# Moving the four state products of group 0 one period later, next to those of group 1

## The chip, the cores and the metric

The kernel runs on one core of a Trainium2 chip. The metric is the device time of one execution in microseconds (us). A profile comes with one execution; its span (first to last instruction) is shorter than the time of the same execution (for example 795.4 and 797.42). PE is the matmul engine, PEld its weight loads, DVE the vector engine, ACT the activation engine, POOL the general engine, and SP the engine that issues the DMAs.

## The reference, cut to what matters

The program is a pre-norm attention with a running memory, followed by a gated MLP. The attention works in 4 segments of 512 tokens and 32 heads of width 32:

```python
for s in range(N):
    p = softmax(qs @ ks^T * scale + mask); a_dot = p @ vs
    a_mem = (phi(qs) @ M) / (phi(qs) @ z + 1e-06)
    outs.append(g * a_mem + (1 - g) * a_dot)
    M = M + phi(ks)^T @ vs          # the "state products"
    z = z + phi(ks).sum(rows)
```

The state products of segment s are used first in segment s+1. The kernel takes 8 groups of 4 heads per segment; one step of the main loop, here "period n", makes the logits of group n, the P·V products and the state products of group n-1, and the Q and K projections of group n+1. So group 0's state products have about six periods (over 45 us) before anybody needs them.

## The kernel before: what the change touches

Instructions go to one queue per engine in the order in which they are recorded. A helper derives the waits; every instruction is issued from one of its lines, which is why the profile says L209 everywhere. It tracks PSUM by whole bank, SBUF in cells of 32 bytes. PQK holds phi(Q) and phi(K) of a group; PK (pk in the profile) is phi(K) after a DMA transpose, and it is the weights of the state products. The logits of a group are made in three rounds, 0 to 2; ACT takes the exp of each round and POOL applies the causal mask. The layer norm's rstd (rs in the profile) is made on POOL too.

```python
MSUM = cb("msum", [128, NQ, 132], F32)
PVX = PS[:, 4:6, :]...[:, 0:688]        # P.V results: bank 4 and columns 0..175 of bank 5
STB = PS[:, 5, 176:308]                 # state products, bank 5
# [...] head of the program: the last loads before the loop, all on SP's one queue
for tc in range(4, 8):
    x_load(tc)
sp.dma_start(WK[:, :, 256:D], wcols(A_wk, 256, D))     # 1.5 MB
sp.dma_start(WQ[:, :, 256:D], wcols(A_wq, 256, D))     # 1.5 MB
phi_exp(0)
phi_max(0)                              # ends with the DMA transpose PK[0] <- PQK[0]
# [...]
def pv(n, cqs=range(4)):
    # [...] P.V matmuls
    if 3 in cqs:
        state(n)                        # 4 matmuls, weights PK[n % 3]
        norm(n)                         # DVE: reads banks 4 and 5, then state_sum(n)
# [...]
def state_sum(n):
    # [...]
    if s == 0:
        dve.tensor_copy(MSUM[:, c, :], STB)
    # [...] three POOL operations: mask with g, fold into MZB
# [...] period n
logits(n, 0); fill(f1)                  # f1: K projection of group n+1
if n > 0: pv(n - 1, range(3))
logits(n, 1)
if n > 0: pv(n - 1, (3,))               # last P.V part, then state and norm
bg_pop()                                # layer-norm statistics on DVE
fill(f2)                                # Q projection of group n+1, and its eviction on DVE
logits(n, 2)
```

The softmax here doesn't subtract the row's maximum and nothing guards it: scores larger than these inputs give would overflow.

## Time and profile before

| | before |
|---|---|
| time, median of the first 3 runs | 796.97 us (796.62 to 797.53) |
| span of the profile | 795.4 us |
| PE busy | 784.7 us |
| DVE busy | 380.0 us |
| one steady period of segment 0 | 7.60 us |

These are lines of the page of the kernel before: the span, the busy time by engine, and the chain of waits by engine and by line.

```profile
span 795.4 us, 13019 instructions
...
PE 784.7 (99%) x5565; PEld 378.3 (48%) x5657; DVE 380.0 (48%) x745; ACT 295.6 (37%) x347; POOL 173.8 (22%) x329
...
PE 94%; DVE 3%; DMA 2%; issue 1%
```

PE bounds the kernel. The chain in order of time (start, duration, what) shows one long piece that is not PE:

```profile
12.30 7.25 PE ps L209 x33
19.55 10.92 DMA pk<-pqk
30.98 7.55 PE ps L209 x83
...
38.59 7.55 PE ps L209 x83
```

The 10.92 us are the time from issue to landing of the transpose of pk of group 0. They are not lost time: PE works under most of them. What is lost is read from the timeline of PE (start, duration, engine, line, operation, output and inputs, count, idle time before):

```profile
29.19 0.57 PE L209 MATMUL ps<-v,e 128*128 128x33 bf16 x16
30.52 0.41 PE L209 MATMUL ps<-v,pk 128*128 128x132 bf16 x4 [0.76 <-DMA pk<-pqk]
30.98 1.67 PE L209 MATMUL ps<-xnT,wq 128*128 128x512 bf16 x7
...
37.72 0.56 PE L209 MATMUL ps<-v,e 128*128 128x33 bf16 x16
38.14 0.40 PE L209 MATMUL ps<-v,pk 128*128 128x132 bf16 x4
...
42.25 0.39 PE L209 MATMUL ps<-qk 32*128 32x512 bf16 x4
```

In period 2 the state products start 0.42 us after the last P·V part. In period 1 it is 1.33 us, so 0.91 us are lost. Two lines of period 2 show how close DVE is to PE (the Q eviction, then the weight load of the first logits of period 3, which need it):

```profile
41.46 0.64 DVE L209 TENSOR_TENSOR qk<-ps,rb 128x512 bf16<-128x512 f32 x1
...
42.24 0.10 PEld L209 LDWEIGHTS ps<-qk 32*128 32x128 bf16 x4 [0.42 <-DVE qk L209]
```

The eviction ends at 42.10 and PE goes on at 42.25. The 0.42 us is idle time of PEld, not of PE: the matmuls of the V projection run until then.

### The profile page before, as it was taken

To read this page: it belongs to the slowest core of one execution; us is meant where nothing else is said; L and a number is where in the kernel's file an instruction comes from. 1 tells how busy PE (TensorE), PEld (TensorE's weight loads), DVE (VectorE), ACT (ScalarE), POOL (GpSimd) and SP (SyncE) were. 2 spreads that over 40 slices of the span, in tenths; PEclk is the share of its full clock that TensorE was granted. 3 is DMA by queue.
4 is the path that set the end of the run, shared out by engine and by line. 5 is a ranking of instruction groups with operands and counts; after the bars stand their busy time and mean duration, and the time that the engine had idled before them with its cause. 6 is when DMAs were issued, how large, how long until landed. Compare 5 with 4: busy or idle time off the path is not lost.

```text
span 795.4 us, 13019 instructions
## 1 busy us (share of the span) xinstructions
PE 784.7 (99%) x5565; PEld 378.3 (48%) x5657; DVE 380.0 (48%) x745; ACT 295.6 (37%) x347; POOL 173.8 (22%) x329
## 2 busy tenths in 40 slices
PE   8999999999999999999999999999999999999998
PEld 3445455554554455455544444444444444444444
DVE  7664689679954765744562000053234323323332
ACT  5777877887787675133333333100000000000000
POOL 4554565566553331100230000000000000000000
DMA  9762555353415425411116000640270143021003
GB/s 296 175 160 60 94 81 121 87 103 84 110 22 126 114 65 136 125 47 54 54 54 132 1 1 0 220 92 7 79 133 1 33 108 78 1 59 54 1 7 86
DMA packets 125002, 64.83 MB, mean 82 GB/s; under 512 B 94992, under 2 KB 113936, under 8 KB 124944
## 3 DMA queue, kind: packets, MB, share of 16 engines
q1 hardware_dynamic: 124944, 63.99, 33.7%
q8 instruction: 44, 0.72, 0.4%
q14 instruction: 14, 0.11, 0.1%
HBM read 32.51 MB, written 8.39 MB: 51 GB/s over the span
## 4 chain that ended last, share of the span: by engine, by line
PE 94%; DVE 3%; DMA 2%; issue 1%
PE ps L209 94%; DMA pk<-pqk 1%; DVE stats L209 1%; DMA xch<-in_A_x_dram 0%; DVE hch L209 0%; DVE otok L209 0%; DVE lno L209 0%; DVE pqk L209 0%; DVE ta L209 0%; DVE xnT L209 0%; DVE rd L209 0%; DVE mv L209 0%; DVE etmp L209 0%; DVE rdm L209 0%; DVE upd L209 0%
## 5 line engine op out<-in xcount | busy, mean ns | idle before, releaser
L209 PE MATMUL ps<-wspT,z 128*128 128x512 bf16 x878 | 193.1, 379 | 0.9
L209 ACT ACTIVATE e<-ps 128x2048 bf16<-128x2048 f32 (+1 forms) x96 | 152.7, 1590 | 42.4 <-PE ps L209 42.3
L209 PEld LDWEIGHTS ps<-wspT,z 128*128 128x128 bf16 x896 | 87.7, 98 | 105.7
L209 DVE TENSOR_TENSOR tmpg<-ps,brow 128x512 f32<-128x512 f32 x56 | 38.7, 691 | 196.7 <-DMA brow<-in_B_b_sp_dram 103.7
L209 POOL TENSOR_SCALAR_AFFINE_SELECT e<-e 128x512 bf16<-128x512 bf16 x128 | 90.3, 717 | 126.2 <-ACT e L209 125.9
L209 PE MATMUL ps<-win,hnT 128*128 128x448 bf16 x512 | 98.4, 352 | 0.0
L209 PE MATMUL ps<-w_out,yT 128*128 128x512 bf16 (+2 forms) x453 | 96.9, 372 | 0.5
L209 PE MATMUL ps<-hnT,win 128*128 128x512 bf16 x439 | 96.2, 379 | 0.5
L209 PEld LDWEIGHTS ps<-win,hnT 128*128 128x128 bf16 x512 | 49.7, 98 | 46.4 <-issue 0.2
L209 PEld LDWEIGHTS ps<-w_out,yT 128*128 128x128 bf16 x462 | 44.7, 98 | 52.3
L209 PEld LDWEIGHTS ps<-hnT,win 128*128 128x128 bf16 x448 | 43.8, 98 | 52.8
L209 PE MATMUL ps<-xnT,wk 128*128 128x512 bf16 x234 | 59.6, 380 | 1.2
L209 PE MATMUL ps<-wv,xnT 128*128 128x512 bf16 x255 | 59.2, 380 | 0.3 <-ACT xnT L209 0.2
L209 ACT ACTIVATE z<-ps 128x448 bf16<-128x448 f32 x60 | 32.5, 543 | 69.4 <-PE ps L209 69.4
L209 PE MATMUL ps<-wo,oT 128*128 128x512 bf16 x254 | 57.7, 379 | 0.1
L209 ACT ACTIVATE z1T<-ps 128x512 bf16<-128x512 f32 x56 | 33.4, 597 | 63.3 <-PE ps L209 63.3
L209 DVE TENSOR_TENSOR fin<-fin,ps 128x512 bf16<-128x512 bf16 (+2 forms) x33 | 22.2, 671 | 71.3 <-DMA fin<-out_dram 39.9
L209 PE MATMUL ps<-xnT,wq 128*128 128x512 bf16 x225 | 53.9, 379 | 1.8 <-issue 0.2
L209 DVE BATCH_NORM_STATS2 zst<-z 128x6 f32<-128x448 bf16 x64 | 38.9, 620 | 30.1 <-ACT z L209 30.1
L209 PEld LDWEIGHTS ps<-v,e 128*128 128x128 bf16 x1280 | 38.8, 96 | 14.0 <-issue 6.5
L209 PE MATMUL ps<-v,e 128*128 128x33 bf16 x1280 | 42.2, 178 | 0.0
L209 DVE TENSOR_TENSOR yT<-tmpg,z1T 128x512 bf16<-128x512 f32 x56 | 38.8, 692 | 1.9
(86 smaller groups left out, 611.8 us busy)
## 6 DMA issues: line engine op xcount, KB each, us to landing
xch<-in_A_x_dram SPq DMA_DIRECT2D x16, 256.0 KB, 3.5
xr<-in_A_x_dram SPq DMA_DIRECT2D x16, 256.0 KB, 4.0
out_dram<-hch SPq DMA_DIRECT2D x16, 256.0 KB, 2.4
fin<-out_dram SPq DMA_DIRECT2D x16, 256.0 KB, 2.8
out_dram<-fin SPq DMA_DIRECT2D x31, 128.0 KB, 1.7
win<-in_B_w_in_dram SPq DMA_DIRECT2D x4, 896.0 KB, 5.1
w_out<-in_B_w_out_dram SPq DMA_DIRECT2D x1, 3584.0 KB, 12.8
win<-in_B_w_in_dram SPq DMA_DIRECT2D x3, 1024.0 KB, 5.1
```

What stands on the lines that cost most here:

```text
L209: ins = getattr(e, op.name)(*op.args, **op.kw)
```

## The change

The intent is to let PE do other work where it waits for pk of group 0. The four matmuls, their copy out of PSUM and three POOL operations move from period 1 to period 2, behind those of group 1. Group 0's results get columns of their own (the same bank 5 nevertheless). The stride of MSUM grows to a multiple of 32 bytes, so that neighbouring groups share no cell.

```diff
-    MSUM = cb("msum", [128, NQ, 132], F32)
+    MSUM = cb("msum", [128, NQ, 136], F32)
-    STB = PS[:, 5, 176:308]
+    STB = [PS[:, 5, o:o + 132] for o in (176, 308)]
 # pv
         if 3 in cqs:
-            state(n)
+            if n:
+                state(n)
+            if n == 1:
+                state(0)
             norm(n)
 # norm
-        state_sum(n)
+        if n:
+            state_sum(n)
+        if n == 1:
+            state_sum(0)
 # state, state_sum: STB becomes STB[n == 0]; MSUM[:, c, :] becomes MSUM[:, c, 0:132]
 # [...]
```

More of the change, by code (lines that the diff above doesn't have):

```diff
@@ L606, in state @@
         for tcl in range(4 if s < NSEG - 1 else 0):
-            pe.matmul(STB, PK[n % 3][:, tcl, :], V[:, tcl, 4 * c:4 * c + 4, 0:33], start=(tcl == 0), stop=(tcl == 3))
+            pe.matmul(STB[n == 0], PK[n % 3][:, tcl, :], V[:, tcl, 4 * c:4 * c + 4, 0:33], start=(tcl == 0), stop=(tcl == 3))
     def state_sum(n):
@@ L613, in state_sum @@
         if s == 0:
-            dve.tensor_copy(MSUM[:, c, :], STB)
+            dve.tensor_copy(MSUM[:, c, 0:132], STB[n == 0])
         else:
-            dve.tensor_copy(UPD[n % 2][:], STB)
-            pool.tensor_tensor(MSUM[:, c, :], MSUM[:, c, :], UPD[n % 2][:], ALU.add)
-        pool.tensor_tensor(DGM[:], MSUM[:, c, :].rearrange("p (i d) -> p i d", d=33), MASKG[:, c, :, :], ALU.mult)
+            dve.tensor_copy(UPD[n % 2][:], STB[0])
+            pool.tensor_tensor(MSUM[:, c, 0:132], MSUM[:, c, 0:132], UPD[n % 2][:], ALU.add)
+        pool.tensor_tensor(DGM[:], MSUM[:, c, 0:132].rearrange("p (i d) -> p i d", d=33), MASKG[:, c, :, :], ALU.mult)
         pool.tensor_tensor(HALF2[:], DGM[:, 0:2, :], DGM[:, 2:4, :], ALU.add)
```

## The prediction

> **What bounds the kernel now.** TensorE: the page has PE busy 784.7 of 795.4 us, and the chain of waits is 94% PE. A steady period of segment 0 lasts 7.60 us, 7.55 of them matmuls back to back. One piece of the chain that is not PE is large: "DMA pk<-pqk", 10.92 us from 19.55. It does not cost 10.92 us, as PE works under nearly all of it. The timeline of PE in period 1 has P·V of group 0 (last part) at 29.19, its state products only at 30.52 (released by DMA pk<-pqk), the Q projection at 30.98. One period later P·V to state takes 0.42 us (37.72 to 38.14). So the stall is 1.33 - 0.42 = 0.91 us.
>
> The transpose of pk is issued at 19.55 and lands 10.9 us later (median of all 24: 2.4), behind 1.5 MB loads of wk and wq on the same queue; wq lands at 29.2. The Trainium skill, "DMA: Bandwidth & Descriptors", section "Two DMAs through the same engine are not ordered", says that within one queue of an engine descriptors start in order; 10.9 against 2.4 us agrees.
>
> **What the change does.** Four matmuls move from period 1 to just behind those of group 1 in period 2, where both transposes have long landed (30.5 and 31.0, against 38). Nothing is added on PE. Their DVE copy (0.28 us, 0.20 start to start) and three POOL operations (1.16 us together) move along. The results get columns of their own, in the same PSUM bank 5. The stride 136 ends false sharing between neighbouring groups, which costs no wait now.
>
> - Period 1: the 0.91 us stall goes; 0.45 us of products move on (neutral).
> - New limits there: the Q projection could start at 29.63; wq landed at 29.20. Round-2 logits would be ready at 31.25; the exp that frees their banks ends at 31.19. Close; I allow 0.05 us.
> - Period 2: the normalisation waits for both products (the kernel guards PSUM by bank), as PE's next work does; but DVE makes two copies, +0.20 us, ahead of the Q eviction that gates the next logits. In a steady period that eviction ends at 42.10 and the logits start at 42.25: hardly any slack. Estimate: 0.12 us of new stall (0.05 to 0.2).
> - POOL: +1.16 us in period 2 delays the round-2 mask to about 43.9 (needed after 45) and the layer-norm rstd by 0.7 us; both have slack.
>
> Net: -0.91 + 0.05 + 0.12, about -0.7 us. What follows starts earlier by as much, as loads are issued by engine progress.
>
> **Predicted:** 796.2 us, range 795.3 to 797.2; faster by over 2%: 0.005, within 2%: 0.99, slower: 0.005.
>
> **What would show each step.**
> 1. No idle of PE by DMA pk<-pqk; the chain loses that piece.
> 2. P·V of group 0 to Q projection in period 1: about 0.45 us, not 1.79.
> 3. In period 2 eight state matmuls in a row, about 0.85 us, and two msum copies.
> 4. First logits of period 3 at 41.5 to 41.7 instead of 42.25; later periods 7.60 us as before, the shift constant to the end.
> 5. PEld waits for "DVE qk" 0.1 to 0.2 us longer there.
>
> **What would make it wrong.** The wq load landing after 29.6: the Q projection takes over the wait, gain under 0.5 us. The DVE delay lasting over more periods, as DVE is nearly in step with PE: gain near 0. Run spread (796.62 to 797.53) exceeds the effect, so medians may hide it. An error in bank 5 would show in the result, not in the time.

## The result

| | before | after |
|---|---|---|
| time, median of 6 runs | 796.79 us (796.33 to 797.53) | 796.80 us (796.49 to 797.13) |
| ratio | | 1.0000, 95% interval 0.9987 to 1.0013 |
| span of the profile | 795.4 us | 795.1 us |

A ratio is the mean time of one kernel's fast runs over that of the other's of the same rounds, so not quite the ratio of the medians. The interval is 1 us wide on either side: the predicted -0.7 us lies inside it, and so does zero. The times alone can't decide; the profile must be read.

Page of the kernel after:

```profile
span 795.1 us, 13111 instructions
...
PE 789.9 (99%) x5657; PEld 378.4 (48%) x5657; DVE 379.3 (48%) x745; ACT 295.6 (37%) x347; POOL 172.1 (22%) x329
...
PE 96%; DMA 2%; DVE 1%; ACT 0%; SPq 0%; issue 0%
```

(PE "busy" is 5 us higher, but 92 more matmul records are in this trace, 5657 against 5565, while both have 5657 weight loads: records are missing before, it is not more work.) The chain, in order of time:

```profile
14.85 0.04 issue
14.89 15.18 DMA wq<-in_A_wq_dram
30.06 0.04 issue
30.11 11.79 PE ps L209 x108
```

The timeline of PE, the same places as before:

```profile
29.42 0.56 PE L209 MATMUL ps<-v,e 128*128 128x33 bf16 x16
30.11 1.90 PE L209 MATMUL ps<-xnT,wq 128*128 128x512 bf16 x8
...
37.08 0.57 PE L209 MATMUL ps<-v,e 128*128 128x33 bf16 x16
37.49 0.63 PE L209 MATMUL ps<-v,pk 128*128 128x132 bf16 x8
37.96 1.89 PE L209 MATMUL ps<-xnT,wq 128*128 128x512 bf16 x8
...
41.94 0.40 PE L209 MATMUL ps<-qk 32*128 32x512 bf16 x4
```

And DVE and PEld in period 2:

```profile
39.27 0.49 DVE L209 COPY msum<-ps 128x132 f32<-128x132 f32 x2
...
41.25 0.64 DVE L209 TENSOR_TENSOR qk<-ps,rb 128x512 bf16<-128x512 f32 x1
...
41.93 0.10 PEld L209 LDWEIGHTS ps<-qk 32*128 32x128 bf16 x4 [0.53 <-DVE qk L209]
```

Three things are seen. The wait for pk is gone. In its place the Q projection of period 1 waits for the wq load: it starts 0.69 us after the last P·V part, where 0.41 us would be free of waits. And in period 2 the Q eviction comes later relative to PE, so that the first logits of period 3 wait for it.

For all further comparisons the span is cut into three parts: the **head** H, from the start to the last P·V part of group 0 (29.19 before, 29.42 after); the **middle** M, from there to the first logits of period 3 (42.25 - 29.19 = 13.06 before, 41.94 - 29.42 = 12.52 after); the **tail**, the rest (753.13 in both, from the ends of the spans before they are rounded). The change acts on the middle only, where it won 0.54 us in this pair of profiles. The head, where both kernels are the same instruction for instruction, was 0.23 us longer; the heads of all 14 profiles below spread over 28.99 to 29.72. The tail is the same to 0.01 us: nothing is given back later.

### The profile page after: what moved, and what is told of

Its sections match the earlier page's. It is cut to its first block, busy times and chain, and to the rows that moved or that the text cites. A ratio compares the mean times of both kernels' runs of the same rounds, so it can differ in the third digit from the quotient of the medians.

```text
span 795.1 us, 13111 instructions
## 1 busy us (share of the span) xinstructions
PE 789.9 (99%) x5657; PEld 378.4 (48%) x5657; DVE 379.3 (48%) x745; ACT 295.6 (37%) x347; POOL 172.1 (22%) x329
## 4 chain that ended last, share of the span: by engine, by line
PE 96%; DMA 2%; DVE 1%; ACT 0%; SPq 0%; issue 0%
PE ps L209 96%; DMA wq<-in_A_wq_dram 2%; DMA xch<-in_A_x_dram 0%; DVE stats L209 0%; ACT junk L209 0%; DVE xnT L209 0%; DVE lno L209 0%; SPq L209 0%; ACT xnT L209 0%; DVE mv L209 0%; DVE fin L209 0%
## 5 line engine op out<-in xcount | busy, mean ns | idle before, releaser
L209 PE MATMUL ps<-xnT,wq 128*128 128x512 bf16 x256 | 60.6, 379 | 0.1
```

Source lines behind the costliest of these rows:

```text
L209: ins = getattr(e, op.name)(*op.args, **op.kw)
```

## The experiments

Theory 1: the wait for pk turned into a wait for the load ahead of it on the queue, wq, and 0.1 us goes to the second copy on DVE; what is left is a gain of some tenths, hidden by the spread of runs. Rival A: all is given back in period 2 or later. Rival B, formed on the way: the 0.91 us of the one profile was not typical, so there was less to win than the profile said.

The table has the 14 profiles. "Landing" is when the last of the DMA's 16 completion events came, in us from the start of the span; "ready" is H + 0.41, when PE could go on without a wait; "stall" is what PE then waits for, in kernels of the old order for pk, in those of the new order for wq.

| profile | H | landing wq | landing pk | ready | stall | M | span |
|---|---|---|---|---|---|---|---|
| before | 29.19 | 29.20 | 30.47 | 29.60 | 0.92 | 13.06 | 795.4 |
| before_stride | 29.62 | 28.95 | 30.15 | 30.03 | 0.17 | 12.31 | 795.1 |
| before_copy1 | 29.51 | 30.71 | 31.99 | 29.92 | 2.12 | 15.70 | 798.3 |
| before_copy2 | 28.99 | 28.05 | 28.67 | 29.40 | 0 | 12.13 | 794.2 |
| before_copy3 | 29.19 | 28.09 | 28.55 | 29.60 | 0 | 12.12 | 794.4 |
| before_split | 29.18 | 23.47 | 23.95 | 29.59 | 0 | 12.13 | 794.4 |
| before_split_again | 29.42 | 22.88 | 23.32 | 29.83 | 0 | 12.13 | 794.7 |
| before_dose | 29.12 | 31.79 | 33.07 | 29.53 | 3.59 | 18.57 | 800.8 |
| after | 29.42 | 30.06 | 31.34 | 29.83 | 0.28 | 12.52 | 795.1 |
| after_again | 29.05 | 28.38 | 29.58 | 29.46 | 0 | 12.23 | 794.4 |
| after_copy2 | 29.01 | 28.17 | 29.27 | 29.42 | 0 | 12.23 | 794.4 |
| after_split | 29.30 | 23.14 | 23.59 | 29.71 | 0 | 12.23 | 794.6 |
| after_split_late | 29.08 | 24.14 | 24.64 | 29.49 | 0 | 12.13 | 794.5 |
| after_dose | 29.72 | 31.45 | 32.72 | 30.13 | 1.37 | 13.61 | 796.5 |

(For the split kernels, wq is the first part of its load.) The tail, from unrounded ends, is 753.11 to 753.13 in all but one (753.25, after_split_late). All kernels were correct.

### before_stride: only the new stride

```diff
-MSUM = cb("msum", [128, NQ, 132], F32)
+MSUM = cb("msum", [128, NQ, 136], F32)      # and 0:132 where it is used
```

> The kernel before with only the new stride 136 of msum, the four state products left in period 1. Both theories: no change, ratio 1.000 within 0.0005, since no wait on msum shows in the trace; it measures the spread of a null change. Its profile also gives a second sample of when the wq load and the pk transpose of group 0 land: if they land where they did before (wq 29.2, pk 30.5 us), the 0.91 us stall appears again; if as in the profile after (30.06, 31.3), the stall is about 1.7 us.

Measured: 797.15 us median (796.67 to 798.39, 5 runs), ratio 1.0006 (0.9993 to 1.0018). The stride does nothing that can be told from zero, though the mean missed the stated 0.0005 by a little. The surprise is the profile: on the same order of instructions the stall was 0.17 us, since pk landed 0.3 us earlier and PE got there 0.4 us later. The stall is a race of two arrivals, and it is drawn anew in each execution. This is where rival B came from.

### after_again, after_copy2: the changed kernel again

No edit.

> The changed kernel once more, with more rounds. Theory 1 (the wait for the pk transpose turned into a wait for the wq load, which is next on the same queue, and 0.1 us is given back by the second msum copy): faster than before by 0.3 to 0.7 us, that is a ratio of 0.9991 to 0.9996, and a stall of the Q projection by DMA wq of 0.2 to 0.6 us in the profile. Rival (all is given back somewhere after period 2): ratio 1.000 within 0.0003, and markers late in the trace that do not keep the shift of period 3.

Measured: 796.55 us median (796.46 to 796.68, 5 runs), ratio 0.9996 (0.9983 to 1.0009); before beside it had 796.88. The size is as theory 1 says, but the interval holds zero. In the profile wq had landed 1.1 us ahead of need, and there was no stall, against my expectation of 0.2 to 0.6 us.

> The changed kernel once more: P.V start of group 0 to first logits of period 3 is 12.23 us plus the stall by DMA wq, if wq lands later than P.V start plus 0.36. I expect a stall of 0 to 0.3 us.

Measured: M is 12.23 us, with no stall. So the wq wait that the first profile of the changed kernel showed is in one of its three profiles.

### before_split, after_split: what is needed first is loaded first

```diff
-sp.dma_start(WK[:, :, 256:D], wcols(A_wk, 256, D))
-sp.dma_start(WQ[:, :, 256:D], wcols(A_wq, 256, D))
+sp.dma_start(WK[:, :, 256:512], wcols(A_wk, 256, 512))
+sp.dma_start(WQ[:, :, 256:512], wcols(A_wq, 256, 512))
 phi_exp(0)
 phi_max(0)
+sp.dma_start(WK[:, :, 512:D], wcols(A_wk, 512, D))
+sp.dma_start(WQ[:, :, 512:D], wcols(A_wq, 512, D))
```

> The changed kernel with wk and wq columns 256 to 511 loaded first and columns 512 to 1023 only behind the pk transpose. Theory 1: no wait for wq in period 1; Q projection about 0.2 us after the last P.V starts plus 0.42, that is 0.42 to 0.5 us behind it; time 0.3 to 0.5 us below the changed kernel, 0.7 to 1.1 us below before (ratio 0.9987 to 0.9992). Rival (gain is given back by period 2 or later): no faster than the changed kernel.

> The kernel before with the same split loads, products left in period 1. Theory 1: pk of group 0 lands at about 24 to 26 us, no stall for it, P.V to state 0.42 us; time 0.1 us below the changed kernel with split loads (no second msum copy ahead of the Q eviction), so 0.8 to 1.2 us below before (ratio 0.9985 to 0.9990). If it isn't faster than before, the pk stall in the profile was not worth its 0.91 us at all.

Measured: after_split 796.72 us median, ratio 0.9998 (0.9985 to 1.0012); before_split 796.52 us median, ratio 0.9996 (0.9984 to 1.0009). The times are not 0.7 to 1.2 us below before as I had expected, but 0.16 and 0.31 us in the means (796.74 and 796.59 against 796.90), inside the noise. The profiles are plain. Timeline of PE, before_split:

```profile
29.18 0.56 PE L209 MATMUL ps<-v,e 128*128 128x33 bf16 x16
29.59 0.40 PE L209 MATMUL ps<-v,pk 128*128 128x132 bf16 x4
29.83 1.89 PE L209 MATMUL ps<-xnT,wq 128*128 128x512 bf16 x8
```

The transpose lands at 23.95, more than 5 us ahead of need, and the stall is gone without any change in the order of PE. M is 12.13 us for the old order and 12.23 us for the new one. So with no stall to remove, the change **costs** 0.10 us of middle. And the mean gain of removing the stall looks smaller than 0.91 us, as before_split is only 0.31 us faster; the interval, 0.9984 to 1.0009, doesn't exclude 0.91 us by itself. This speaks for rival B, and against rival A, as the tails are equal.

> The kernel before with split loads, once more. Theory: neither wait exists, so the time is 753.1 us of tail plus 12.13 us plus the head (28.9 to 29.6 us to the last P.V of group 0) plus the constant 2.0 us between span and time: 796.2 to 796.9 us in every run, with no run at 798 or above; mean 0.1 to 0.5 us below the fast runs of before. In the profile: P.V to state 0.41 us, P.V to first logits of period 3 12.13 us. A run above 798 us would show a stall of another origin.

Measured: 796.40 us median (796.25 to 797.00, 5 runs) against 796.91 of before, ratio 0.9995 (0.9981 to 1.0008). One run was 0.1 us above the stated limit of 796.9, none near 798. M was 12.13 again.

### after_split_late: is the 0.10 us the second copy?

```diff
 # norm
-        if n == 1:
-            state_sum(0)
 # main loop
         fill(f2)
+        if n == 2:
+            state_sum(0)
         logits(n, 2)
```

This is the split kernel of the new order; the copy of group 0 now stands behind the Q eviction in DVE's queue.

> The changed kernel with split loads, and the msum copy of group 0 moved behind the Q eviction of period 2. Theory: from the start of the last P.V of group 0 to the first logits of period 3 it takes 12.13 us (as in before_split) instead of the 12.23 of after_split, as the 0.10 us wait of the logits for the Q eviction goes. If the 0.10 us has another cause, 12.23 stays.

Measured: M is 12.13 us. DVE first and then PE, from its timeline:

```profile
40.41 0.64 DVE L209 TENSOR_TENSOR qk<-ps,rb 128x512 bf16<-128x512 f32 x1
40.97 0.28 DVE L209 COPY msum<-ps 128x132 f32<-128x132 f32 x1
...
44.02 0.84 DVE L209 TENSOR_SCALAR lno<-xch,mv,rs 128x1024 bf16<-128x1024 bf16 x1 [1.57 <-POOL rs L209]
44.78 0.68 DVE L209 TENSOR_TENSOR qk<-ps,rb 128x512 bf16<-128x512 f32 x1
```

```profile
39.37 1.90 PE L209 MATMUL ps<-wv,xnT 128*128 128x512 bf16 x8
41.21 0.40 PE L209 MATMUL ps<-qk 32*128 32x512 bf16 x4
...
48.94 0.39 PE L209 MATMUL ps<-qk 32*128 32x512 bf16 x4
```

The eviction now ends 0.16 us ahead of the logits. That settles the 0.10 us of the middle: it was the second copy ahead of the eviction. But nothing is won in all. The next logits come 7.73 us later (41.21 to 48.94) where a period takes 7.60, and the tail is 753.25 us instead of 753.13: the 0.10 us come back one period later. As the timeline reads, the later copy delays POOL's three operations and then rs; DVE waits for rs, and its K eviction ends only at 45.46, after PE's products (45.10), so that the normalisation starts late. This is one profile, and no run tests that reading.

### before_copy1 to before_copy3: how large is the stall of the kernel before?

No edit.

> The kernel before, unchanged, for one more sample of its stall. In the first profile the stall was 0.91 us, in the copy with another msum stride 0.17 us. From the start of the last P.V of group 0 to the first logits of period 3: 12.13 us plus the stall, whatever the stall is; stall = landing of pk plus 0.05 us minus (start of that P.V plus 0.41), if positive. I expect a stall between 0 and 1.2 us.

> As before_copy1: the kernel before, unchanged, another sample of its stall; P.V start of group 0 to first logits of period 3 is 12.13 us plus the stall, the stall between 0 and 1.2 us by the landing of pk.

> As before_copy1: one more sample; with the first profile and the stride copy five samples in all, whose mean stall I expect at 0.3 to 0.6 us, well below the 0.91 us of the first profile.

Measured: 800.38, 796.29 and 796.49 us; the stalls were 2.12, 0 and 0 us. With the first profile and before_stride, five draws of one order: 0, 0, 0.17, 0.92, 2.12 us, mean 0.64 and median 0.17. The mean is just above the range I gave, carried by one draw that is above the stated 1.2 us; M of that draw also breaks my formula of 12.13 plus the stall by 1.45 us. Timeline of PE in before_copy1:

```profile
29.51 0.56 PE L209 MATMUL ps<-v,e 128*128 128x33 bf16 x16
32.04 0.62 PE L209 MATMUL ps<-v,pk 128*128 128x132 bf16 x4 [1.96 <-DMA pk<-pqk]
32.45 3.16 PE L209 MATMUL ps<-xnT,wq 128*128 128x512 bf16 x8
```

The eight matmuls of the Q projection took 3.16 us where they take 1.89. The busy times by stretches (stretch, length, busy time and count of PE, PEld, DVE, ACT and POOL, then the granted PE clock, DMA share, GB/s) say why:

```profile
31.50:32.00 0.50, 0.00 (x0) 0.00 (x0) 0.00 (x0) 0.01 (x1) 0.42 (x1) 0.60 0.66 140
34.00:35.00 1.00, 1.00 (x3) 0.29 (x2) 0.97 (x3) 0.00 (x0) 0.75 (x2) 0.50 0.00 0
35.00:36.00 1.00, 1.00 (x9) 0.32 (x8) 0.96 (x3) 0.11 (x1) 0.26 (x2) 0.99 0.00 0
```

The granted clock fell to one half during the idle time and stayed there until 35.0 us. From 32.04 to 35.0 PE thus worked 2.96 us at half clock, which makes an estimated loss of 1.48 us, against the 1.45 measured. This stall cost more than its length. In the same profile the K projection ahead of the stall had already waited 0.45 us for wk, a wait that the change doesn't touch.

### before_dose, after_dose: make the DMAs late on purpose

```diff
+sp.dma_start(WO[:, :, 0:512], wcols(A_wo, 0, 512))   # 1 MB between wk and wq; loaded again later
 sp.dma_start(WQ[:, :, 256:D], wcols(A_wq, 256, D))
```

> The kernel before with 1 MB more put on the queue between the wk and the wq load (half of wo, which is loaded again later, so the result stays right). Theory 1 (the stall is the landing of pk minus the time PE gets there): at the early loads' rate, about 0.37 MB per us, wq and pk of group 0 land about 2.8 us later, pk at 32.5 to 34; stall of PE by DMA pk in period 1 of 2.7 to 4 us; time 2.4 to 3.5 us above before, ratio about 1.003 to 1.0045. If PE gets by without it: ratio 1.000.

> The changed kernel with the same extra 1 MB. Theory 1: now the Q projection waits for wq, which lands 1.1 to 1.3 us ahead of pk, so the change is worth that distance less 0.1 us: 0.9 to 1.2 us faster than before_dose in time, and still 1.4 to 2.4 us slower than before. Rival (the change removes the DMA wait for good): as fast as the changed kernel without the extra load, 3 us below before_dose.

Measured: before_dose 801.27 us median (799.56 to 802.90, 4 runs), ratio to before 1.0054 (1.0037 to 1.0070); after_dose 798.59 us (798.50 to 800.94, 4 runs), ratio 1.0030 (1.0013 to 1.0047). Here the change is worth 2.1 us by the means (801.25 - 799.15), about double what I expected; before_dose is 4.3 us above before (796.94), over the 2.4 to 3.5 expected, and after_dose 2.2 us, as expected. Timelines of PE, before_dose and then after_dose:

```profile
29.12 0.56 PE L209 MATMUL ps<-v,e 128*128 128x33 bf16 x16
33.12 0.62 PE L209 MATMUL ps<-v,pk 128*128 128x132 bf16 x4 [3.43 <-DMA pk<-pqk]
33.53 3.62 PE L209 MATMUL ps<-xnT,wq 128*128 128x512 bf16 x8
```

```profile
29.72 0.56 PE L209 MATMUL ps<-v,e 128*128 128x33 bf16 x16
31.50 1.69 PE L209 MATMUL ps<-xnT,wq 128*128 128x512 bf16 x7 [1.21 <-DMA wq<-in_A_wq_dram]
```

This is theory 1 in the open: the old order waits for pk, the new one for wq, which lands 1.28 us ahead (31.79 and 33.07 in before_dose). The mechanism was right and the size was not, for the reason that before_copy1 had shown: in before_dose M is 18.57 = 12.13 + 3.59 of stall + 2.85 us at a lowered clock (the stretches show 0.66 in 32 to 33 us, 0.50 from 33 to 39, 0.93 in 39 to 40), while after_dose, with 1.21 us idle, kept clock 1.00 and its M is 13.61 = 12.23 + 1.37 + 0.01. The record gives the mean granted clock of each run, and it tells the same: the one run of before_dose that kept 1.000 took 799.56 us, 1.0 us above the three of after_dose that did (798.50 to 798.67), which is the size expected (0.9 to 1.2); the others of before_dose have 0.996 to 0.998. One run of after_dose took 800.94 us, and its clock was 0.998, as in before_copy1: so its clock fell too. There is no profile of it, and what made its wait longer stays open.

## Why the prediction came out as it did

The time lay in the range (796.8 in 795.3 to 797.2), and "within 2%" was right. That hit says nothing of the mechanism, as the range also holds the time of the unchanged kernel (796.79). The stated gain of 0.7 us was not confirmed: the first comparison gave 0.0 with an interval of 1 us on either side. Point by point:

- **"So the stall is 1.33 - 0.42 = 0.91 us"** and "the 0.91 us stall goes". Right for that profile (the table has 0.92), mis-sized as a term of the sum. Five profiles of that order gave 0, 0, 0.17, 0.92 and 2.12 us. I had read one draw of a race between DMA and PE as a constant.
- **Behind the loads on the same queue.** In all profiles wk, wq and pk landed in the order of issue, and the time from issue to landing of pk fell from 9.0 to 12.6 us to 3.5 to 5.2 us in the split kernels. The Trainium skill, "DMA: Bandwidth & Descriptors", section "Two DMAs through the same engine are not ordered", says that descriptors within one queue of one engine start in order; these landings agree, though they show completions and not starts.
- **"I allow 0.05 us" for new limits in period 1.** The wait for wq was 0.28, 0 and 0 us in three profiles. That the load could take over the wait stood under "what would make the prediction wrong"; it happens in executions where DMA is late, the same ones in which pk is late. The change gains the distance of the two landings then, not the whole stall.
- **"Estimate: 0.12 us of new stall"** in period 2. Right: 0.10 us in every profile of the changed kernel, and after_split_late showed the cause. The normalisation did wait for both products, as I had said of the guard by bank: its first operation started at 38.16, the eight products ended at 37.49 + 0.63 = 38.12. The Trainium skill, "PSUM — Partial Sum Buffer", section "PSUM bank collisions raise a hardware error", asks for a guard by bank and quadrant, by bank as the simple form. No run here shows a collision, as none leaves the guard out. The guard's wait itself cost PE nothing: DVE was idle for 1.21 us before that operation, against 0.97 us in the kernel before, but after_split_late keeps that wait (1.21) and has the short middle of 12.13 us.
- **POOL has slack**: right for this change; its later rstd made DVE wait (1.6 us instead of 0.5), but nothing of it reached PE. The slack is small: in after_split_late rs ended 14.91 us after the last P·V part of group 0, against 14.57 in after_split, and the next period was 0.13 us longer.
- **"The shift constant to the end"**: right, the tails of both kernels agree to 0.02 us in all their profiles.
- **"First logits of period 3 at 41.5 to 41.7"**: measured 41.94, of which 0.23 us is a longer head and 0.28 us the wait for wq.

What the change is worth on average can only be estimated. The split kernels of the old order, which have no stall, were 0.31 and 0.40 us faster than before in the means of the two chips (796.59 against 796.90, 796.55 against 796.95). That is what the stall costs in timed runs, give or take an interval of 1 us. Less 0.10 us for the copy and less the wait for wq, an estimate for the change is 0.2 us, of 797. The direct means say much the same: after was 0.01 us faster in the first comparison and 0.35 us in after_again. These are noisy means; the times do not prove it. What the profiles do show is what the change does: it removes the part of the wait that lies between the landings of wq and pk, and it cost 0.10 us in each. Of the versions run, before_split, which only reorders loads, has the shortest middle (after_split_late has the same, but a longer tail) and takes away the reason for the change; it isn't proven faster in time.

Open: why the landings of the same queue differ by up to 3.4 us from one execution to the next (28.55 to 31.99 for pk), and whether the profile, which is taken in one execution, draws late landings more often than other runs: of the 32 timed runs of before none took over 797.68 us, and one of the five profiled executions of that order took 800.38. The wk load varies along with pk (23.86 to 26.71 in the same five profiles), so most of the cause is ahead of wq.

## What to carry to other kernels

A wait for a DMA in one profile is one draw: take several profiles before you put its length into a sum. When work that waits for a load moves away, look at the load ahead of it on the queue, since the next wait is there and what is won of the wait is the distance of the two landings (more, as in the dose runs, only where the longer wait also lowered the clock). Reordering the loads by need left neither wait in four profiles, at no cost that they show, where shifting the work put 0.10 us onto an engine that runs in step with the bottleneck. And follow a saving past its own period: that of after_split_late was gone one period later.

## What the Trainium skill lacked or had wrong

- "TensorE: Matmul & The Clock Gate", section "HAM oscillation — how this bites in real kernels", gives as the rule no idle gaps of PE above about 3.4 us, and the section "What's actually happening" lets the clock fall after at least one idle window of about 3.4 us. In before_copy1 a gap of 1.96 us was enough for a fall to 0.50. By the clock of the stretches it fell about 1.5 us after the last matmul (0.60 in 31.5 to 32.0 makes 0.4 us at one half, so at 31.6; P·V ended at 29.51 + 0.56 = 30.07). In before_dose it fell 2.6 us after the last matmul (0.66 in 32 to 33, so at 32.3; P·V ended at 29.68), so the delay isn't fixed. A gap of 1.21 us in after_dose did not do it. The measurement decides: the safe gap was below 2 us here. The stretches at one half, 3.4 us in before_copy1 and 6.8 us in before_dose, do fit one and two of its windows.
- The same page works out the penalty of a lowered clock only for a loop with a gap in every step. Here a single gap cost 1.45 us on top of 2.12 us, and 2.85 us on top of 3.59 us.
- "DMA: Bandwidth & Descriptors" says nothing about how much the landing of a given transfer varies between executions of one kernel: 9.0 to 12.6 us from issue for the pk transpose behind the same queue, in eight profiles.
